# A fused windowed-attention and mixture-of-experts kernel: a new hand-written order, the last unit in two expert halves, end tiles in another PSUM pool

## The chip, the cores and the metric

The kernel runs on one core of a Trainium2 chip. The metric is the device time of one execution in microseconds (us), the median of several runs. A profile of one execution gives the span from the first to the last instruction, and what each engine did: TensorE (PE, its weight loads apart as PEld), VectorE (DVE), ScalarE (ACT), GpSimd (POOL), and SyncE (SP), which only issues DMAs here.

## The reference

There are two stages. The first is attention with 4 batches, 8 heads, 768 positions and head width 64, in which a query sees only the first 8 keys and the last 96, with a linear bias by distance:

```python
keep = is_global | is_local                      # first 8 keys, or 0 <= rel < 96
scores = scale * (q @ k^T) - slopes[h] * dist
a = softmax(where(keep, scores, -1e9));  x = (a @ v) as (B, 768, 512)
```

The second is a layer of 4 attention experts over x. Each expert projects q, k and v (512 to 64), does causal attention over all 768 positions and projects back to 512. A gate picks two experts for each position:

```python
logits = x @ w_gate;  w = softmax(top 2 of logits)
out[pos] = sum over the 2 chosen experts e of  w_e * (causal_softmax(x wq_e, x wk_e) @ (x wv_e) @ wo_e)[pos]
```

The inputs q, k and v have 6.3 MB each, the output has 6.3 MB, all float32.

## The kernel before

The work is cut into 24 units: a unit is 128 positions of one batch, six to a batch (`NU = B * NT`). For each unit there is a fixed set of stages, each a small function, and a string `ORDER` lists all calls of all units, one slot for each. A slot is a stage's two letters, the unit, and, where there is a choice, the engine or queue: `kc5g` casts k of unit 5 on GpSimd (`g`; `v` is VectorE, `a` ScalarE, `s` the SP queue). A loop walks through the string and emits the instructions in exactly that order (`tc.manual_schedule()`), so each engine gets its own instructions as one queue, in the order of the string, and an instruction that waits holds up everything behind it on its engine. The framework sets the semaphores.

The stages, with lines of the kernel before:

- `lk`, `lq`, `lv`: load 256 KB of k, q or v of a unit (L238), on the SP queue or ScalarE's. `wi0` to `wi3` load wk, wq, wv and wo (512 KB each), `wi4` the gate.
- `kc`, `qc` (L258), `vc`, `vx` (L267): cast to float16. `wc` casts weights.
- `tk`, `tq`: transpose k and q on PE (L283), and after q one copy of both out of PSUM (L285).
- `sa`, `sb`: local scores of a unit, bias and scores in one PSUM tile (L345, L352), then the exponential on ScalarE (L355). They need k of this unit and q of this and the next.
- `gs`, `vs`, `vg`, `va`, `vb`: scores of the global keys, and the values (L366, L381); `vb` ends with the normalization on VectorE (L388, L390). `tx` transposes the result (L402).
- `pk`, `pq` (L414), `pv` (L428): the experts' projections. `ro` are the steps of the gate.
- `ca`, `cb`, `cc`: causal scores (L459) and exponentials (L462). `ma` masks the diagonal block on GpSimd (L474).
- `za`, `zb`: causal values of experts 0 and 1, and of 2 and 3 (L487), then on VectorE reciprocal (L494), product with the gate (L496) and scaling (L498). `tz` transposes that (L509, copy L512), `ou` projects it (L519), copies it out of PSUM (L522) and stores 256 KB (L523).
- `xb`, `xm`, `xc`, `xk`, `xs`, `xi`, `az`: masks, biases and zeros made once at the start. `wm5` is five matmuls whose result is never used (L248), which keep TensorE busy. `ck` sums up whether all softmax sums were in a safe range; a branch at the end goes to a slower general path where they were not (not taken here). `bh` marks where the branch may be hinted at.

PSUM has eight banks of 2 KB for each partition. `psS` holds two tiles of two banks (scores), `psZ` one tile of two banks (values), `psT` two tiles of one bank (transposes, projections, outputs). A tile of a pool is given out again when the engines that read it are done. So `za` of a unit can't begin before the scaling L498 of the unit before has read the `psZ` tile.

Of the kernel before, what the change touches and what calls it, by code (L numbers as in the profile page):

```python
# [22 lines left out]
def kernel(  # L23
# [59 lines left out]

    def bias_constants(_):
        V.tensor_copy(rel[:, :], rel_i[:, :])
        ge = const.tile([P, W], F32, name="ge")
        V.tensor_scalar(ge[:, :], rel[:, :], 0.0, None, op0=Alu.is_ge)
        lt = const.tile([P, W], F32, name="lt")
        V.scalar_tensor_tensor(lt[:, :], rel[:, :], float(NL), ge[:, :],
                               op0=Alu.is_lt, op1=Alu.mult)  # L90
        V.tensor_scalar(lt[:, :], lt[:, :], -1.0, -NEG, op0=Alu.add, op1=Alu.mult)
        V.tensor_scalar(rel[KB:P, :], rel[KB:P, :], slopes[1] / slopes[0], None, op0=Alu.mult)
        for p in range(NP):
            V.scalar_tensor_tensor(biasT[:, p, :], rel[:, :], -slopes[2 * p] / sc1, lt[:, :],
                                   op0=Alu.mult, op1=Alu.add)
# [137 lines left out]
    s16s, zs_, x16s, routing, zss, zts, tps, ppss, zs2 = ({} for _ in range(9))  # L233
# [243 lines left out]
    def causal_values(u, i):  # L477
# [6 lines left out]
        z_ps = zs2[u][:, 0, 0:E * VW].rearrange("r (e d) -> r e d", e=E)  # L484
        for e in range(i * E // 2, (i + 1) * E // 2):
            for ci in range(n):
                mm(z_ps[:, e, :], lhsT=a2[:, e % 2, (e // 2) * n + ci, :],  # L487
                   rhs=held("v2buf", b * NT + ci)[:, e, :], start=(e == 0 and ci == 0), stop=True,
                   skip_group_check=True)
# [8 lines left out]
        V.tensor_tensor(zss[u][:, :, :], z_ps[:, :, 0:Hd],  # L498
                        ce[:, :].unsqueeze(2).to_broadcast([P, E, Hd]), op=Alu.mult)

    def turn_z(u, on):
        zts[u] = pp.tile([P, NEP, P], F16, name="zt")
        if on == "s":
            nc.sync.dma_start_transpose(zts[u][:, :, :],
                                        zss[u][:, :, :].rearrange("r e d -> r (e d)"))
            return
        zt_ps = psT.tile([P, NEP, P], F16, name="ztps", tag="t")
# [6 lines left out]
    def output(u, on):  # L514
        b, ri = divmod(u, NT)
        assert 3 in ready
        o_ps = psT.tile([P, D], F32, name="ops", tag="t")
# [5 lines left out]
        dma(out[b, ri * P:(ri + 1) * P, :], o_sb[:, :])  # L523

# [220 lines left out]
    def branch_hint(_):  # L745
# [8 lines left out]
        "vs": (select_values,), "xb": (bias_constants,), "xi": (half_identities,),  # L754
# [9 lines left out]
    }  # L764
    for slot in ORDER.split():
        stage, *args = stages[slot[:2]]
        if slot[-1].isalpha():
            args.append(slot[-1])
        stage(int(slot[2:].rstrip("agsv")), *args)
# [5 lines left out]
    n_f = const.tile([1, 1], F32)  # L775
    V.reduce_sum(n_f[:, :], n_ps[:, :], axis=Ax.X)
    n_i = const.tile([1, 1], I32)
    V.tensor_copy(n_i[:, :], n_f[:, :])
# [13 lines left out]
xb0 lk0s kc0v lq0s az0v az1g lk1s xi0a xs0v xk0g lq1a wm14 tk0 qc0g lv0s kc1g lk2s lq2s lk3a  # L792
wm5 tq0a lq3s xc0g lv1a lv2s lq4s lk4a qc1v lq5s vc0g vx0g wm4 tk1 tq1v xm0v lk5s wm10 sa0 sb0
wm10 vs0 gi0 wi0a wm2 gs0 lk6s kc2v qc2v tk2 tq2v wm3 gs1 lq6s wm7 vg0 kc3g va0 vb0 vc1g vx1v
qc3a sa1 az2g sb1 tk3 tq3v tx0v wi1a vg1 az3g qc4a vc2g kc4g vx2v wm2 va1 wm4 sa2 sb2 vb1 qc5g
gs2 kc5a wc0g tk4 tq4v tx1v az4v lv3s vg2 va2 lv4s vb2 sa3 sb3 tk5 tq5v wm6 tx2v kc6a lq7s wi2a
qc6v wm4 sa4 sa5 tk6 vc3g tq6v pk0 sb4 sb5 wc1v pk1 wm2 gs3 wm2 pq0a vx3v pq1a gi1 vg3 vc4g
vx4g wi4s lv5s va3 vb3 lk7a ca0 ma0 pk2 pq2v tx3v ca1 vg4 va4 vb4 lq8s ca2 pk3 pq3a lk8s vc5v
vx5v cb2 vg5 wc2g lv6s kc7g lq9s pv0v pv1v lq10a lk9s qc7g qc8g kc8g ca3 cb3 tk7 lv7s tq7v pv2v
ro0 va5 sa6 tk8 tq8v tx4v vc6g vx6g lk10a lk11s vb5 sb6 gs4 lv8s ro0 pv3v pk4 qc9g pq4v ro0 ro0  # L800
lq11s lq12a ma1 vs1 lk12s lk13a sa7 tx5v kc9g pv4v kc10g ma2 vg6 va6 ro0 vb6 ca4 tk9 tq9v pk5
lk14s lq13s lv9a pq5v cb4 tx6v sb7 vc7v qc10g qc11a vx7g vc8g tk10 tq10v pv5v kc11g kc12g lq14a
qc12g cc4 vg7 va7 lq15s vb7 ro0 ro0 pk6 pq6a tk11 tq11v vx8g sa8 sb8 tx7v lk15s kc13g kc14g za0
qc13g zb0 lv10a tk12 tq12v gi2 pv6a sa9 sa10 ro1 ro1 lv11s lv12s vc9v vg8 va8 vb8 pk7 pq7a vx9g
tk13 tq13v lk16s lk17s gs5 ca5 qc14g lq16s tz0v za1 lq17s ro1 tk14 tq14v zb1 tx8a ro1 sb9 vc10g
vx10g sb10 kc15a pv7v pv8v vc11g vg9 va9 kc16a vb9 sa11 sa12 tz1v ro1 lq18s kc17v pk8 pq8a za2
ro1 tk15 zb2 sb11 sb12 qc15g tq15v tx9a vc12g vx11g vg10 va10 lk18s vx12g qc16g qc17v vb10 gs6
vs2 tk16 tq16v wi3s qc18g kc18g tk17 tq17v ma3 cb5 vg11 ma4 lk19s va11 lv13s lv14s cc5 tx10v
lv15s tk18 tq18v vb11 ca6 pv9v pv10a ro1 sa13 ro2 sa14 lq19s lq20s gi3 lq21s wc3g za3 ro2 zb3
ou0v ou1a vc13g ro2 ca7 lq22s ca8 vx13g vg12 ma5 va12 vb12 tx11v pk9 pq9v za4 ro2 lk20s kc19g  # L810
zb4 lk21s lk22s lv16s ma6 tz2a ro2 sb13 sa15 tx12v qc19v qc20g pk10 pq10a vc14g vx14g kc20g ma7
tz3v vg13 vc15g ro2 va13 vb13 lv17a cb8 gs7 ma8 ou2v tk19 tq19v lk23s lv18a za5 sb14 sb15 tz4v
zb5 tx13a pv11v sa16 ro2 sb16 vg14 va14 vb14 pk11 ro3 lv19s lv20a pq11a pv12v sa17 za6 zb6 ro3
ro3 vc16g vx15g vx16g ou3a ou4v qc21v ca9 lv21s cb9 tk20 kc21g tq20v za7 pk12 zb7 pq12a tx14v
vc17g ca10 vx17g ro3 cb10 vg15 va15 qc22g tz5v tz6v vb15 ou5a vc18g vc19g tk21 tq21v sa18 vc20v
sb17 kc22g kc23g za8 zb8 tx15a pk13 pq13v ca11 vg16 cc10 va16 pv13v lv22a pv14v cb11 ma9 vb16
gs8 ou6a pk14 pq14v ca12 vx18g vg17 va17 vb17 ca13 tz7v ro3 pk15 ro3 ro3 vx19v pq15a sb18 vs3
tx16v tx17v za9 zb9 ro4 pk16 lq23s pq16a ou7v ro4 lv23s qc23g cc11 vg18 va18 vc21g vb18 pv15a
tk22 tq22v sa19 sa20 ma10 pv16v ma11 za10 tz8a zb10 sb19 sb20 ro4 ro4 ro4 pv17v tz9v ca14 vg19
va19 vb19 ou8a ou9a vx20v sa21 sb21 ro4 ro4 tk23 tq23v ro5 za11 tx18v zb11 tz10a sa22 sb22  # L820
tx19v ma12 pv18v cb14 vg20 va20 vb20 gs9 ro5 ou10a pv19v ma13 vx21g ca15 ca16 vc22g za12 tz11v
zb12 pk17 pq17v pk18 pq18v ro5 ma14 ro5 vc23g cb15 vx22g vg21 va21 vb21 cb16 ro5 tx20v ro5 ro5
pk19 pq19a za13 zb13 pv20a ro6 sa23 sb23 tx21v vg22 va22 vb22 cc16 tz12v pk20 ro6 pq20a za14
zb14 ou11a ro6 ca17 ca18 tz13v ma15 za15 tz14v vx23g zb15 ro6 ro6 ou12a ou13v cb17 vg23 va23
# [46 lines left out]
```

## Time and profile before

| what | value |
|---|---|
| median of 3 runs | 153.25 us (156.71, 151.09, 153.25) |
| the profiled execution's own time | 152.97 us |
| its span, first to last instruction | 150.8 us, so 2.17 us lie around it |
| busy in the span | PE 140.3 us (93%), DVE 111.4, ACT 108.1, POOL 90.2 |
| TensorE's clock | 0.998 of full speed |
| read and written | 20.98 MB and 6.29 MB |

Busy time counts an instruction from its start to its modelled end; PE's matmuls overlap in the pipeline, so a group of them takes less than the sum. The table of stages gives for each stretch the busy time of each engine (with the number of instructions in brackets), TensorE's clock, the mean share of the DMA engines, and GB/s. The chain of waits follows back from the last instruction what released each step. The timeline gives instructions in order of time, with start and duration.

### The profile page before, as it was taken

The page shows a single profiled execution, that of the slowest core. Times are in us where ns is not written, and L with a number is a line of the kernel's source. Part 1 is how long each engine was busy: PE and PEld are TensorE (multiplying, and loading weights), DVE is VectorE, ACT ScalarE, POOL GpSimd, SP SyncE. Part 2 cuts the span into 40 slices and gives each one's busy share as a digit, 9 for nine tenths or more (in the row PEclk, how much of TensorE's full clock was granted, in tenths as well). Part 3 has the DMA queues.
Part 4 walks back from the last instruction along what each step waited for, and adds up shares of the span by engine and source line. Part 5 has one row for each costly group of instructions (what it writes and reads, how often), then busy time and mean ns, then how long its engine had stood idle before and what let it go on. Part 6 is the DMA issues. An engine that isn't in the chain of part 4 may idle for free.

```text
span 150.8 us, 7217 instructions
## 1 busy us (share of the span) xinstructions
PE 140.3 (93%) x3029; PEld 110.2 (73%) x3029; DVE 111.4 (74%) x348; ACT 108.1 (72%) x176; POOL 90.2 (60%) x254
## 2 busy tenths in 40 slices
PE   5799999999999999999978999999999999999760
PEld 4567778887778888878757778888778878786520
DVE  4838676687899887878863987687787777778850
ACT  4027657778576888888638998887977978989640
POOL 7278351568878988797827899136286345463200
PEclk9999999999999999999999999999999999999999
DMA  4999998999999989899899963415221005013462
GB/s 99 280 252 286 276 261 192 254 247 238 277 282 275 245 201 249 189 256 208 231 240 288 301 166 113 116 43 142 74 77 70 4 19 195 24 51 127 155 263 97
DMA packets 85364, 27.77 MB, mean 184 GB/s; under 512 B 82000, under 2 KB 82000, under 8 KB 85328
## 3 DMA queue, kind: packets, MB, share of 16 engines
q1 hardware_dynamic: 62496, 21.51, 56.6%
q10 hardware_dynamic: 22832, 5.77, 17.1%
q8 instruction: 24, 0.39, 1.0%
q14 instruction: 12, 0.10, 0.2%
HBM read 20.98 MB, written 6.29 MB: 181 GB/s over the span
## 4 chain that ended last, share of the span: by engine, by line
PE 74%; DMA 11%; DVE 4%; POOL 3%; ACT 2%; issue 1%; SPq 1%; ACTq 0%; POOLq 0%; DVEq 0%
PE pps L414 14%; PE cps L459 7%; PE vps L428 7%; PE tp L283 7%; PE ops L519 6%; PE zps L487 6%; PE zps L381 6%; PE sps L345 5%; PE zps L248 4%; DMA kf<-in_k_dram 4%; DMA vf<-in_v_dram 4%; PE xps L402 3%; PE sps L352 3%; DMA qf<-in_q_dram 3%; PE zps L366 2%; PE ztps L509 2%
## 5 line engine op out<-in xcount | busy, mean ns | idle before, releaser
L462 ACT ACTIVATE a<-cps 128x1024 f16<-128x1024 f32 (+1 forms) x48 | 42.2, 917 | 8.3 <-PE cps L459 6.6
L355 ACT ACTIVATE abuf<-sps 128x636 f16<-128x636 f32 (+1 forms) x48 | 30.6, 686 | 12.8 <-PE sps L352 10.1
L267 POOL CAST vbuf<-vf 64x256 f16<-64x256 f32 x76 | 31.0, 408 | 8.4 <-DMA vf<-in_v_dram 5.2
L474 POOL TENSOR_SCALAR_AFFINE_SELECT a<-a 128x256 f16<-128x256 f16 x48 | 18.3, 409 | 5.1 <-ACT a L462 4.8
L285 DVE COPY kqT<-tp 128x1024 f16<-128x1024 f16 x23 | 15.7, 688 | 6.6 <-PE tp L283 6.1
L390 DVE TENSOR_TENSOR x<-zps,rinv 128x512 f16<-128x512 f32 x24 | 16.6, 691 | 0.8
L487 PE MATMUL zps<-v2buf,a 128*128 128x65 f16 x336 | 16.0, 193 | 0.6 <-DVE zs L498 0.5
L345 PE MATMUL sps<-biasT,ident 64*64 64x318 f16 (+1 forms) x192 | 14.5, 305 | 1.4 <-ACT abuf L355 1.3
L381 PE MATMUL zps<-vbuf,abuf 64*128 64x65 f16 x704 | 15.5, 189 | 0.0
L258 POOL CAST s16k<-kf 128x512 f16<-128x512 f32 x17 | 10.3, 612 | 8.7 <-DMA kf<-in_k_dram 8.3
L487 PEld LDWEIGHTS <-a 128*128 128x128 f16 x336 | 13.3, 97 | 2.1 <-DVE zs L498 0.9
L381 PEld LDWEIGHTS <-abuf 64*128 64x128 f16 x704 | 14.0, 94 | 1.1 <-issue 0.2
L414 PE MATMUL pps<-xT,wk 128*128 128x128 f16 x192 | 14.7, 219 | 0.0
L414 PE MATMUL pps<-xT,wq 128*128 128x128 f16 x192 | 14.5, 219 | 0.0
L248 PE MATMUL zps<-ident 128*128 128x240 f16 x75 | 12.8, 316 | 1.7 <-POOL ident masks.py:199 1.6
L428 PE MATMUL vps<-wvg,xT 128*128 128x260 f16 x96 | 13.9, 275 | 0.0
L459 PEld LDWEIGHTS <-kq 64*128 64x128 f16 x336 | 9.7, 94 | 5.8 <-issue 4.4
L459 PE MATMUL cps<-kq,kq 64*128 64x128 f16 x240 | 13.8, 218 | 0.0
L519 PE MATMUL ops<-wo,zt 128*128 128x512 f16 x48 | 13.5, 380 | 0.4 <-DVE zt L512 0.4
L352 PE MATMUL sps<-kqT 64*64 64x159 f16 (+2 forms) x384 | 13.8, 223 | 0.0
L258 POOL CAST s16q<-qf 128x512 f16<-128x512 f32 x15 | 9.4, 630 | 5.1 <-DMA qf<-in_q_dram 4.9
L414 PEld LDWEIGHTS <-wk 128*128 128x128 f16 x192 | 11.5, 98 | 0.8
(113 smaller groups left out, 286.4 us busy)
## 6 DMA issues: line engine op xcount, KB each, us to landing
out_dram<-osb SPq DMA_DIRECT2D x24, 256.0 KB, 2.3
qf<-in_q_dram SPq DMA_DIRECT2D x20, 256.0 KB, 5.6
kf<-in_k_dram SPq DMA_DIRECT2D x19, 256.0 KB, 5.7
vf<-in_v_dram SPq DMA_DIRECT2D x17, 256.0 KB, 5.5
vf<-in_v_dram ACTq DMA_DIRECT2D x7, 256.0 KB, 4.7
kf<-in_k_dram ACTq DMA_DIRECT2D x5, 256.0 KB, 4.9
qf<-in_q_dram ACTq DMA_DIRECT2D x4, 256.0 KB, 4.5
w<-in_moe_wk_dram ACTq DMA_DIRECT2D x1, 512.0 KB, 5.3
```

What stands on the lines that cost most here:

```text
L248: mm(current["z"][:, 0, 4 * P - 2 * NC:4 * P].rearrange("r (a n) -> r a n", a=2), lhsT=ident[:, :], rhs=ident[:, 0:NC].unsqueeze(1).to_bro ...
L258: copies[on](s16s[nm, u][:, :, :], fs[nm, u][:, :, :])
L267: copies[on](o[hf * KB:(hf + 1) * KB, c, :, 0:Dh], fs["v", u][c * KB:(c + 1) * KB, hf * HG:(hf + 1) * HG, :])
L345: mm(s_ps[o, hh, 0:2 * w].rearrange("r (c n) -> r c n", c=2), lhsT=ident2[r, :], rhs=biasT[r, p, 0:w].unsqueeze(1).to_broadcast([KB, 2, w] ...
L355: S_.activation(as_[u][:, :, g, :].rearrange("r h (c n) -> r h c n", c=2)[:, :, :, 0:w], s_ps[:, :, 0:2 * w].rearrange("r h (c n) -> r h c ...
L381: mm(zs_[u][:, hf, hq * VW:(hq + 1) * VW], lhsT=as_[u - prev][r, hq % 2, hq // 2, at:at + P], rhs=held("vbuf", u - prev)[r, c, hq, :], sta ...
L414: mm(p_ps[:, i, ep, :], lhsT=w[:, ko, ep, :, :].rearrange("r a d -> r (a d)"), rhs=xT[:, ko, :], start=(i == 0 and ep == 0 and ko == 0), s ...
L428: mm(v_ps[:, :], lhsT=xT[:, ko, :], rhs=wvg16[:, ko, :], start=(ko == 0), stop=(ko == NK - 1))
L459: mm(s_ps[:, e2, i, :], lhsT=kqs[b * NT + ci][r, 0, ep, :], rhs=kqs[u][r, 1, ep, :], start=(i == 0), stop=True, skip_group_check=True)
L462: S_.activation(a2[:, :, 4 * c:4 * c + len(part), :], s_ps[:, :, 0:len(part), :], func=Exp, scale=sc2)
L487: mm(z_ps[:, e, :], lhsT=a2[:, e % 2, (e // 2) * n + ci, :], rhs=held("v2buf", b * NT + ci)[:, e, :], start=(e == 0 and ci == 0), stop=Tru ...
L519: mm(o_ps[:, :], lhsT=zts[u][:, ep, :], rhs=wo16[:, ep, :], start=(ep == 0), stop=(ep == NEP - 1))
```

## The change

There are five edits, and all slots of `ORDER` are in a new sequence.

1. The last unit (23): `za` and `zb` now write the two banks of its `psZ` tile, one for experts 0 and 1 and one for 2 and 3, and each half is divided, weighted and scaled by itself. `tz23` and `ty23` transpose the halves one by one, `ou23` and `oy23` project them, in column halves of 256 each into the two banks of a `psS` tile. The left half is copied by VectorE and stored through the SP queue, the right half copied by ScalarE and stored through ScalarE's queue.
2. `end_tile`: the transposes of units 22 on and the outputs of units 21 on take their PSUM tile from `psS` and not from `psT`.
3. The bias constants come in two parts, `xb` and `xp`, with other work between them.
4. The final sum goes straight to an integer, one VectorE instruction fewer. `bh0` stands first.
5. `ORDER`: the first loads are `v0 q0 k0 q1 k1 k2 k3`, all on SP, and of the 19 loads that ScalarE's queue issued 4 are left. Masks are made before the first casts. There are 64 unused matmuls instead of 75, and they lie elsewhere. Casts and copies change engines here and there.

```diff
+        const_of["lt"] = lt
+
+    def pair_biases(_):
         for p in range(NP):
...
         if i == 0:
             zs2[u] = current["z"] = psZ.tile([P, 2, 4 * P], F32, name="zps2", tag="z")
-        z_ps = zs2[u][:, 0, 0:E * VW].rearrange("r (e d) -> r e d", e=E)
+        last = u == NU - 1
+        nz = E // 2 if last else E
+        z4 = zs2[u][:, :, 0:nz * VW].rearrange("r a (e d) -> r a e d", e=nz)
         for e in range(i * E // 2, (i + 1) * E // 2):
             for ci in range(n):
-                mm(z_ps[:, e, :], lhsT=a2[:, e % 2, (e // 2) * n + ci, :],
...
+                mm(z4[:, e // nz, e % nz, :], lhsT=a2[:, e % 2, (e // 2) * n + ci, :],
...
-        if i == 0:
+        if i == 0 and not last:
             return
...
+        z, e = (z4[:, i], slice(i * nz, i * nz + nz)) if last else (z4[:, 0], slice(0, E))
+        rinv = rinv2[:, b, ri, e]
+        V.reciprocal(rinv, z[:, :, Hd])
+        ce = pp.tile([P, nz], F32, name=f"ce{nz}")
+        V.tensor_mul(ce[:, :], rinv, wts[u // NH][:, ri % NH, e])
+        V.tensor_tensor(zss[u][:, e, :], z[:, :, 0:Hd],
+                        ce[:, :].unsqueeze(2).to_broadcast([P, nz, Hd]), op=Alu.mult)
+
+    def end_tile(u, first, shape, dtype, name):
+
+        if u < first:
+            return psT.tile(shape, dtype, name=name, tag="t")
+        return psS.tile(shape, dtype, name=name, tag="s")
...
-        zt_ps = psT.tile([P, NEP, P], F16, name="ztps", tag="t")
+        zt_ps = end_tile(u, NU - 2, [P, NEP, P], F16, "ztps")
...
-        o_ps = psT.tile([P, D], F32, name="ops", tag="t")
+        o_ps = end_tile(u, NU - 3, [P, D], F32, "ops")
...
+    def turn_last_z(ep, on):
+
+        zt_ps = psT.tile([P, P], F16, name="ztps1", tag="t")
+        nc.tensor.transpose(zt_ps[:, :],
+                            zss[NU - 1][:, 2 * ep:2 * ep + 2, :].rearrange("r e d -> r (e d)"),
+                            ident[:, :])
+        zts[ep, "last"] = pp.tile([P, P], F16, name=f"zt{ep}", bufs=1)
+        copies[on](zts[ep, "last"][:, :], zt_ps[:, :])
+
+    def last_output(ep):
+
+
+        b, ri = divmod(NU - 1, NT)
+        if ep == 0:
+            outs["last"] = [psS.tile([P, 2, D], F32, name="ops1", tag="s")] * 2
+        for i in range(2):
+            c = slice(i * D // 2, (i + 1) * D // 2)
+            o_ps = outs["last"][i][:, i, 0:D // 2]
+            mm(o_ps, lhsT=zts[ep, "last"][:, :], rhs=wo16[:, ep, c], start=(ep == 0),
+               stop=(ep == NEP - 1), skip_group_check=True)
+        if ep == 0:
+            return
+        for i, (copy, queue) in enumerate(((V.tensor_copy, dma), (S_.copy, S_.dma_start))):
+            c = slice(i * D // 2, (i + 1) * D // 2)
+            o_sb = pp.tile([P, D // 2], F32, name=f"osb{i}", bufs=1)
+            copy(o_sb[:, :], outs["last"][i][:, i, 0:D // 2])
+            queue(out[b, ri * P:(ri + 1) * P, c], o_sb[:, :])
...
-xb0 lk0s kc0v lq0s az0v az1g lk1s xi0a xs0v xk0g lq1a wm14 tk0 qc0g lv0s kc1g lk2s lq2s lk3a
-wm5 tq0a lq3s xc0g lv1a lv2s lq4s lk4a qc1v lq5s vc0g vx0g wm4 tk1 tq1v xm0v lk5s wm10 sa0 sb0
-wm10 vs0 gi0 wi0a wm2 gs0 lk6s kc2v qc2v tk2 tq2v wm3 gs1 lq6s wm7 vg0 kc3g va0 vb0 vc1g vx1v
-qc3a sa1 az2g sb1 tk3 tq3v tx0v wi1a vg1 az3g qc4a vc2g kc4g vx2v wm2 va1 wm4 sa2 sb2 vb1 qc5g
-gs2 kc5a wc0g tk4 tq4v tx1v az4v lv3s vg2 va2 lv4s vb2 sa3 sb3 tk5 tq5v wm6 tx2v kc6a lq7s wi2a
-qc6v wm4 sa4 sa5 tk6 vc3g tq6v pk0 sb4 sb5 wc1v pk1 wm2 gs3 wm2 pq0a vx3v pq1a gi1 vg3 vc4g
...
-ma21 pk23 pq23a ro7 za19 zb19 ca22 ou15v tz17v cb22 za20 cc22 tz18v ro7 ro7 ou16a zb20 ou17v
-ck0 ck1 ca23 bh0 cb23 za21 tz19v zb21 ou18v cc23 tz20v ma22 za22 zb22 tz21a ou19a ou20v ma23 za23 tz22v
-zb23 ou21a ou22a tz23v ou23a ck2
+bh0 xb0 xm0v lv0s xk0v xi0a lq0s qc0a lk0s xs0g az0g kc0v wm29 tk0 lq1s lk1s az1v az2g xp0 vc0a
+qc1g lk2s lk3s vx0v kc1g lq2a tq0a kc2v wm12 tk1 tq1v lq3s xc0v kc3g lk4s wm2 vs0 wm9 sa0 sb0
+gi0 lq4s tk2 lv1s qc2g qc3v qc4g lv2s tk3 tq2v gs0 vc1g wm1 tq3v vx1g lq5a gs1 wm3 gs2 vg0 va0
+kc4v vb0 lk5s qc5g wi0s kc5g sa1 sb1 wi1s az3v vc2v lv3a tk4 sa2 vx2g wm4 sb2 tx0a az4v lv4s
+tq4v vg1 wc0g wc1g va1 vb1 wi4s sa3 sb3 wi2s lv5s tk5 lk6s tq5v lq6s lk7s vg2 wm2 va2 vb2 sa4
+sa5 tx1v tx2v lq7s vc3v lq8s gs3 pk0 pk1 vx3v vc4g vx4v lk8s sb4 wm2 pq0a pq1a vg3 vc5g va3 vb3
...
+ro7 ou17v ca23 cb23
+tz19v ma21 za21 zb21 cc23 ou18v tz20v ck0 ck1 ma22 za22 ma23 zb22 tz21a ou19v ou20a za23 zb23
+tz22a ou21a tz23v ou22a ty23v ck2 ou23 oy23
```

## The prediction

> **What bounds the kernel now.** I read the page's busy shares first (PE 93%), then the chain of waits, then the table of stages to see where the missing 7% and the unused matmuls lie, then the timeline of the first 30 us and the last 10.
>
> ```profile
> PE 140.3 (93%) x3029; PEld 110.2 (73%) x3029; DVE 111.4 (74%) x348; ACT 108.1 (72%) x176; POOL 90.2 (60%) x254
> PE 74%; DMA 11%; DVE 4%; POOL 3%; ACT 2%; issue 1%; SPq 1%; ACTq 0%; POOLq 0%; DVEq 0%
> ```
>
> TensorE is the bound: 74% of the chain. Next, the stages (first all work, then the unused matmuls of L248 alone):
>
> ```profile
> 0.00:10.00 10.00, 7.10 (x42) 5.19 (x43) 5.13 (x21) 2.78 (x4) 5.68 (x27) 1.00 0.89 202
> 10.00:20.00 10.00, 9.95 (x198) 7.37 (x197) 7.45 (x19) 5.60 (x11) 6.42 (x16) 1.00 1.25 280
> 20.00:30.00 10.00, 9.68 (x234) 7.96 (x230) 7.46 (x18) 7.36 (x14) 4.29 (x11) 1.00 1.09 229
> 30.00:70.00 40.00, 40.00 (x951) 32.31 (x946) 33.01 (x95) 31.23 (x52) 32.45 (x81) 1.00 1.07 242
> 70.00:80.00 10.00, 8.62 (x205) 7.03 (x203) 7.48 (x22) 5.79 (x11) 5.69 (x16) 1.00 1.01 241
> 80.00:140.00 60.00, 59.88 (x1351) 47.48 (x1351) 46.11 (x155) 51.60 (x81) 34.91 (x104) 1.00 0.38 112
> 140.00:151.00 11.00, 5.07 (x64) 2.83 (x63) 4.77 (x21) 3.75 (x7) 0.77 (x2) 0.97 0.44 165
> ...
> 0.00:10.00 10.00, 5.65 (x26) 3.69 (x27) 1.00 0.89 202
> 10.00:20.00 10.00, 5.01 (x37) 3.04 (x35) 1.00 1.25 280
> 20.00:30.00 10.00, 2.10 (x14) 1.20 (x14) 1.00 1.09 229
> ```
>
> Useful work in the first three stretches is 7.10 - 5.65 = 1.45, 4.94 and 7.58 us. So of the first 30 us TensorE loses 16.0. It loses 1.4 in 70 to 80, and 5.9 in the last 11 us. Between, it is full. Hence the change can earn in three places only, and elsewhere a new order only shuffles full work.
>
> **What the Trainium skill says.** (1) "DMA: Bandwidth & Descriptors", "Issuing engines are not separate DMA queues": DMAs of all issuing engines run on the same 16 DMA engines, and a second issuing engine saves only sequencer time. No stretch of this trace has one queue alone under full load, so it is not shown here; I take it that moving 15 loads from ScalarE's queue to SP costs no bandwidth. (2) Same page, "Anatomy of one DMA": about 2.0 us of a DMA are fixed (stated for another issuing path). The trace agrees in size: the last stores of 256 KB land after 2.0 us. Halving a store therefore saves little. (3) "PSUM — Partial Sum Buffer", "PSUM bank collisions raise a hardware error": two engines must be kept apart on one bank, while different banks are free. In the changed kernel's list of instructions the framework orders by tile, not by bank, as I use below. (4) "TensorE: Matmul & The Clock Gate", "What's actually happening": after an idle window of about 3.4 us the clock falls to half. In every stretch up to 140 us it is 1.00 here, so fewer unused matmuls are safe while gaps stay shorter.
>
> **The start (edits 3 and 5).** Loads: 4.82 MB arrive in the first 20 us (2.02 and 2.80), that is 18.4 tiles of 0.262 MB, some 0.95 us each once running. The old list loads wk (issued at 13.20 us on ScalarE's queue) beside q5 and ahead of k5, and then has no use for wk until 25.87 us; GpSimd meanwhile stands waiting for q5, and later for v3:
>
> ```profile
> 19.38 0.61 POOL L258 CAST s16q<-qf 128x512 f16<-128x512 f32 x1 [2.76 <-DMA qf<-in_q_dram]
> 25.61 0.86 POOL L267 CAST vbuf<-vf 64x256 f16<-64x256 f32 x2 [4.24 <-DMA vf<-in_v_dram]
> 25.87 0.61 PE L414 MATMUL pps<-xT,wk 128*128 128x128 f16 x8
> ```
>
> In the new one q5 and k5 are tiles 14 and 15 (17 us, against 19.4 for q5), wk 16 and 17 (19 us), wq 18 and 19 (21 us).
>
> First scores `sa0`: now 11.03 us. They need k and q of units 0 and 1. New: v0 q0 k0 q1 k1 come in this order, so k1, the fifth, lands near 7.3 (its cast starts at 8.05 now). But VectorE makes the mask first (seven steps, 2.3 us at 10.40 to 12.76 now) and three small memsets, so the cast of k0 moves from 5.21 to about 7. Then tk0, tq0, ScalarE's copy of 1.01, 12 unused matmuls, tk1, tq1, VectorE's copy of 0.69: `sa0` at about 11.3. Price +0.3.
>
> From `sa0` to the first projection L414: 14.84 us now. In that stretch the old list has 38 unused matmuls, the new one 10. Ten of 240 columns take 1.20 us with the last one's tail, 0.1 each. So 28 x 0.1 = 2.8 us of filler go. Whether real work can take the place depends on data: the mask and the cast behind it held tk2 until 13.62 now (VectorE 10.40 to 13.85 without a pause), and that is done beforehand; q5 and k5 come earlier, as said. The useful work before the first L414 is the same but for tk6, tq6 (0.46, now after it) and gs3 (0.25, now before): not a gain, only a shift. From the first L414 to the end of pq1 (3.3 us now) two unused matmuls fewer: 0.2. So by the count 2.8 + 0.2 - 0.3 = 2.7. Following the chain by hand instead (scores of units 1 to 4 at 14.3, 15.4, 17.9 and 19.6 against 16.12, 18.96, 22.11 and 24.82, then L414 when wk is cast at 20 to 21) gives 4.7, without any hitch. From below it is 0, if the waits are just exposed. I take **3.0**. The three ends are kept for the range.
>
> ScalarE loses 15 loads of about 0.4 us of issue each and gains six casts of v (0.35); VectorE and GpSimd keep their load within 1 to 2 us. These engines are at 60 to 74%, so this is worth nothing by itself.
>
> **The middle.** The 1.4 us of 70 to 80 come from this chain:
>
> ```profile
> 61.97 0.28 DVE x L390
> 62.26 5.98 DMA vf<-in_v_dram
> 68.29 0.40 POOL vbuf L267
> ...
> 73.47 4.66 DMA qf<-in_q_dram
> ```
>
> A load of v waits for a buffer, lands 6 us later, and the values wait for its casts. In the new list lv13 to lv15 stand about one unit earlier, but all of them on SP, behind whatever waits there. Between 0 and 1.4 saved; I take 0.5. What is late next is GpSimd, 80% busy in 30 to 70.
>
> **The tail (edits 1, 2, 4).** Counted from the start of the scaling L498 of unit 22, 142.20 now:
>
> ```profile
> 142.20 0.42 DVE L498 TENSOR_TENSOR zs<-zps,ce 128x256 f16<-128x256 f32 x1
> 142.75 0.52 PE L487 MATMUL zps<-v2buf,a 128*128 128x65 f16 x12
> 144.22 0.42 DVE L498 TENSOR_TENSOR zs<-zps,ce 128x256 f16<-128x256 f32 x1
> 145.33 0.29 DVE L512 COPY zt<-ztps 128x256 f16<-128x256 f16 x1 [0.68 <-PE ztps L509]
> 146.32 0.59 ACT L522 COPY osb<-ops 128x512 f32<-128x512 f32 x1 [0.86 <-PE ops L519]
> ```
>
> The last copy ends at 146.91, 4.71 after. New, in the same count: za23 at 0.55, 12 matmuls, reciprocal at 1.11, 0.41 more to the scaling, which takes 0.29 for half the width (0.42 less 128 columns), end 1.81. Now the added wait: zb23 writes the other bank, but of the same tile, and the new list has it wait for VectorE. Behind it are tz22, ou21 and all the rest of TensorE. So zb23 starts at 1.94 (now the two halves follow each other, but for unit 22's transposes); its scaling ends at 3.20. Then tz22, ou21, ou22 (which waits for ScalarE's copy of zt22), ty23 at 3.65, its copy until 4.16; `ck2` on VectorE until 4.5; oy23 done at 4.6; VectorE's copy of 256 columns, 0.42, until 5.05. ScalarE's copy of the other half waits for VectorE's in the new list, again one tile: 0.37, until 5.46. That is 0.75 later. Given back: at most 0.3 by half the store (an estimate from 128 KB at the page's 436 GB/s), and 0.15 for the integer step, which lies beside the store. The waits of 0.2 that edit 2 removes (transposes behind an output copy) are already in this count. `ck0`, `ck1` (1.04 us) stand one unit later, the same on either side of it. `bh0` leaves the branch hint at the same second place in each engine's list: nothing. Price of the tail **+0.5**, between -0.3 and +1.0.
>
> **Sum**, against the profiled execution's own 152.97: -3.0 - 0.5 + 0.5 = -3.0, so 150.0. The median of the runs is 153.25, 0.3 above that execution. A change of about 2% is what a measurement of this kernel can tell from none.
>
> **Rivals.**
> A, the whole chain comes true: 4.7 at the start, 1.4 in the middle, tail 0: 146.9. For it: DMA is at 164 GB/s in 24 to 26 us now, so there is idle transfer to use. Against: TensorE's order is fixed, every hitch counts.
> B, the lead is given back: TensorE reaches batches 1 and 2 earlier than their loads do, and stands where it doesn't now. Start 1.5, middle -0.5 (a loss), tail +0.5: 152.5. For it: DMA share is above 1.0 until 90 us; against: 27 tiles have come by 30 us in both lists, and projections can fill in.
> C, slower: head of the line on SP. All but 4 loads now go through one queue in order, and stores too; a store there waits up to 9.3 us for its copy. The two transfers of the chain above (5.98 + 4.66 = 10.6) cost TensorE only 1.4 today, so 9.2 are covered by other work. If half of the cover (4.6) goes and the early loads stall likewise so that only 0.5 of the start is left: 152.97 - 0.5 + 4.6 + 0.5 = 157.6. It decides from some 3.1 us of new idle time between 40 and 100 us beyond what the start brings.
>
> **Chances.** Forecast 0.40 (its own range 148.4 to 151.5), A 0.15, B 0.28, C 0.17. Faster by over 2% means under 150.2: A, a good half of the forecast, a little of B, 0.44. Slower is C, 0.17. The rest is 0.39. The range goes from A's 146.5 to 154.5, above B, and leaves out most of C.
>
> **What would show it.** Right: first L414 at 22 to 23 us, some 25 unused matmuls between 10 and 30 us; TensorE's useful work up to 30 us near 17 instead of 14.0; in the tail TensorE idle about 0.9 us between za23 and zb23, and the two halves of the last copy one after the other. Wrong: first L414 later than 24.5; more than 2 us of TensorE idle between 30 and 130 (B, C), with POOL or TensorE waiting for loads; or a clock below 1.00 before 30 us.

## The result, and the profile after

The changed kernel takes 172.57 us (median of four runs, 171.36 to 173.95) beside 153.39 for the kernel before. Some executions of either kernel take a few per cent longer than its others, and the ratios here leave those out: 1.131 times as long, 95% interval 1.108 to 1.155. The prediction, 150.0, had the wrong sign. The profiled execution of after took 171.36 us, with a span of 169.7 against 150.8.

From the profile's page of after, first the busy times, then the chain of waits by engine:

```profile
PE 145.6 (86%) x3020; PEld 113.4 (67%) x3020; DVE 113.8 (67%) x359; ACT 109.9 (65%) x182; POOL 89.0 (52%) x241
PE 44%; DMA 25%; SPq 13%; POOL 4%; DVE 4%; ACT 2%; issue 2%; POOLq 0%; DVEq 0%; ACTq 0%
```

TensorE held 74% of the chain before and holds 44% now. Transfers and their issue on SP (DMA, SPq) went from 12% to 38%. So loads hold nearly as much of the chain as TensorE. The stages (columns as before: PE, its weight loads, DVE, ACT, POOL, clock, DMA share, GB/s), then the unused matmuls (`wm`) alone:

```profile
0.00:10.00 10.00, 7.23 (x50) 5.52 (x51) 7.05 (x25) 4.11 (x7) 5.42 (x23) 1.00 1.01 176
10.00:20.00 10.00, 9.10 (x169) 6.29 (x170) 6.05 (x19) 5.89 (x12) 3.37 (x8) 1.00 1.35 220
20.00:30.00 10.00, 8.38 (x175) 6.16 (x175) 6.87 (x18) 4.16 (x7) 5.86 (x14) 0.83 1.08 203
30.00:70.00 40.00, 33.75 (x731) 26.93 (x729) 25.01 (x73) 24.80 (x43) 23.82 (x55) 0.93 0.97 206
70.00:80.00 10.00, 10.00 (x245) 8.64 (x242) 7.13 (x21) 7.38 (x15) 7.46 (x19) 0.95 1.04 230
...
0.00:10.00 10.00, 6.74 (x41) 5.07 (x41) 1.00 1.01 176
10.00:20.00 10.00, 2.81 (x19) 1.57 (x19) 1.00 1.35 220
20.00:30.00 10.00, 0.96 (x4) 0.25 (x4) 0.83 1.08 203
```

Three things stand here. From 30 to 70 us TensorE was full before (40.00) and is idle for 6.25 now, part of the rest at a lower clock. Loads come at 203 to 220 GB/s where they came at 229 to 280. And in 10 to 20 us the DMA engines are *busier* than before (share 1.35 against 1.25) while they move less. The page counts all packets of 16 engines, and nearly all of them hold 256 bytes, so the time of one packet can be worked out: share x 16 x 256 B / rate. That is 18.3 ns before (1.25 x 4096 / 280) and 25.1 ns after (1.35 x 4096 / 220). A packet of the same size from the same tensor has become slower there. From 30 to 70 us, where the engines are less busy, the same sum gives only 19.3 ns after (0.97 x 4096 / 206) against 18.1 before (1.07 x 4096 / 242).

The first projections, awaited at 22 to 23 us, start later than before (timeline of after):

```profile
27.50 1.05 PE L419 MATMUL pps<-xT,wk 128*128 128x128 f16 x16
```

The end, by the timeline: start of unit 22's scaling, second half of the values, the last two copies.

```profile
157.13 0.42 DVE L507 TENSOR_TENSOR zs<-zps,ce 128x256 f16<-128x256 f32 x1
...
158.91 0.52 PE L494 MATMUL zps<-v2buf,a 128*128 128x65 f16 x12 [0.78 <-DVE zs L507]
...
161.42 0.42 DVE L561 COPY osb<-ops 128x256 f32<-128x256 f32 x1 [0.18 <-PE ops L554]
...
161.88 0.37 ACT L561 COPY osb<-ops 128x256 f32<-128x256 f32 x1 [0.64 <-DVE ones L819]
162.15 0.15 DVE L824 TENSOR_REDUCE n_i<-nps 1x1 int32<-1x3 f32 x1 [0.30 <-PE nps L821]
```

Work ends at 162.3. The span ends at 169.7, so 7.4 us follow the last work; before, it was 150.8 - 146.9 = 3.9. Of the 18.9 us that the span grew, 15.4 lie before the last work and 3.5 after it.

### The profile page after: what moved, and what is told of

Read it like the earlier page. It is cut to its first block, busy times and chain, and to the rows that moved or that the text cites. A ratio compares the mean times of both kernels' runs of the same rounds, so it can differ in the third digit from the quotient of the medians.

```text
span 169.7 us, 7189 instructions
## 1 busy us (share of the span) xinstructions
PE 145.6 (86%) x3020; PEld 113.4 (67%) x3020; DVE 113.8 (67%) x359; ACT 109.9 (65%) x182; POOL 89.0 (52%) x241
## 4 chain that ended last, share of the span: by engine, by line
PE 44%; DMA 25%; SPq 13%; POOL 4%; DVE 4%; ACT 2%; issue 2%; POOLq 0%; DVEq 0%; ACTq 0%
SPq L243 11%; DMA qf<-in_q_dram 10%; DMA kf<-in_k_dram 9%; PE pps L419 8%; DMA w<-in_moe_wq_dram 6%; PE ops L530 6%; PE cps L464 5%; PE zps L494 5%; PE vps L433 4%; PE zps L386 4%; PE tp L288 3%; PE xps L407 2%; PE sps L350 2%; PE sps L357 2%; PE ztps L520 1%
## 5 line engine op out<-in xcount | busy, mean ns | idle before, releaser
L272 POOL CAST vbuf<-vf 64x256 f16<-64x256 f32 x66 | 26.6, 403 | 14.7 <-DMA vf<-in_v_dram 8.8
L263 POOL CAST s16q<-qf 128x512 f16<-128x512 f32 x19 | 11.6, 613 | 14.0 <-DMA qf<-in_q_dram 7.7
L386 PE MATMUL zps<-vbuf,abuf 64*128 64x65 f16 x704 | 16.4, 195 | 0.5 <-POOL vbuf L272 0.5
L263 POOL CAST s16k<-kf 128x512 f16<-128x512 f32 x18 | 11.2, 627 | 9.4 <-DMA kf<-in_k_dram 8.2
L386 PEld LDWEIGHTS <-abuf 64*128 64x128 f16 x704 | 15.0, 97 | 1.6 <-issue 1.1
L288 PE MATMUL tp<-ident,s16k 128*128 128x128 f16 x96 | 10.2, 233 | 6.8 <-POOL s16k L263 6.7
L350 PE MATMUL sps<-biasT,ident 64*64 64x318 f16 (+1 forms) x192 | 15.2, 319 | 0.2 <-ACT abuf L360 0.2
L357 PE MATMUL sps<-kqT 64*64 64x159 f16 (+2 forms) x384 | 14.3, 232 | 0.6 <-DVE kqT L290 0.5
L357 PEld LDWEIGHTS <-kqT 64*64 64x64 f16 x384 | 11.7, 111 | 2.0 <-issue 1.0
L288 PEld LDWEIGHTS <-s16k 128*128 128x128 f16 x96 | 6.4, 103 | 9.8 <-POOL s16k L263 8.3
```

The lines of the kernel that those rows point to most:

```text
L263: copies[on](s16s[nm, u][:, :, :], fs[nm, u][:, :, :])
L272: copies[on](o[hf * KB:(hf + 1) * KB, c, :, 0:Dh], fs["v", u][c * KB:(c + 1) * KB, hf * HG:(hf + 1) * HG, :])
L288: nc.tensor.transpose(tps[u][:, i, p, :], s16[:, p * P:(p + 1) * P], ident[:, :])
L357: mm(s_ps[o, hh, c * w:c * w + n], lhsT=kqT[b][r, 0, p, k0:k0 + KB], rhs=kqT[b][r, 1, p, k0:k0 + n], start=False, stop=True, skip_group_ch ...
L386: mm(zs_[u][:, hf, hq * VW:(hq + 1) * VW], lhsT=as_[u - prev][r, hq % 2, hq // 2, at:at + P], rhs=held("vbuf", u - prev)[r, c, hq, :], sta ...
```

## Experiments

Two differences could touch the rate of the loads: the queues (19 loads on ScalarE's queue before, 4 after; none of the 4 is among the 19, which have all gone to SP) and the buffers. The second comes from edit 4. It drops `n_f`, a constant tile of one number, which takes 32 bytes in each partition; all that is allocated after it moves down by 32 bytes. The buffers of k, q and v start at byte 78336 of a partition before, a multiple of 256, and at 78304 after, 224 past one. Below, "on the line" means that the buffers start at a multiple of 256 bytes, "off the line" that they don't.

### The queues alone, and the offset alone

**e1**: the order before, with its 19 `a` loads turned into `s`.

```diff
-xb0 lk0s kc0v lq0s az0v az1g lk1s xi0a xs0v xk0g lq1a wm14 tk0 qc0g lv0s kc1g lk2s lq2s lk3a
+xb0 lk0s kc0v lq0s az0v az1g lk1s xi0a xs0v xk0g lq1s wm14 tk0 qc0g lv0s kc1g lk2s lq2s lk3s
...
```

> The kernel before with one difference: its 19 loads on ScalarE's queue are issued on SP, at the same places of the order. Theory Q (one queue of 256 B packets carries only some 210 GB/s, against 280 for two): loads fall behind as in the changed kernel, 210 GB/s in 10 to 50 us, TensorE starved, 163 to 173 us. Theory O (the new order itself, its places of loads and casts, starves TensorE; the queue is free of cost): 151 to 155 us, 250 GB/s or more in 10 to 50 us.

**e2**: the converse, in the kernel after the same 19 loads on ScalarE's queue again (`lq1a lk3a lk4a lv1a wi0a` ...), and the other 4 on SP.

> The changed kernel with the 19 loads that ScalarE's queue issued in the kernel before back on that queue (and lq2, lq5, lv3, lv21 on SP, as there), in the new order. Theory Q: 150 to 157 us, 250 GB/s or more in 10 to 30 us and the clock back at 1.00. Theory O: 168 to 174 us.

**e5**: the kernel before with the integer sum of edit 4 and nothing else.

```diff
-    n_f = const.tile([1, 1], F32)
-    V.reduce_sum(n_f[:, :], n_ps[:, :], axis=Ax.X)
     n_i = const.tile([1, 1], I32)
-    V.tensor_copy(n_i[:, :], n_f[:, :])
+    with nc.allow_low_precision("whole numbers"):
+        V.reduce_sum(n_i[:, :], n_ps[:, :], axis=Ax.X)
```

> The kernel before with edit 4's integer sum alone, so without the 32 bytes of the tile n_f; that moves every later buffer in SBUF down by 32 bytes, and the buffers that loads fill from a start at 0 to one at 224 modulo 256. Theory A (a 256 B packet written across a 256 B line of SBUF takes 25 ns and not 18, so that all 16 engines carry at most 218 GB/s): 162 to 172 us, 218 GB/s at most in 10 to 50 us. Theory O (the new order of loads and casts): 151 to 154 us, as the kernel before, less 0.1.

Measured: e1 1.081 times the kernel before (1.069 to 1.093), e2 1.152 (1.141 to 1.162), e5 1.086 (1.076 to 1.097). Stages of e1:

```profile
10.00:20.00 10.00, 9.94 (x189) 7.33 (x188) 6.94 (x19) 5.34 (x11) 4.78 (x13) 1.00 0.93 210
30.00:70.00 40.00, 33.24 (x750) 26.44 (x751) 26.58 (x77) 24.07 (x41) 29.17 (x73) 0.99 0.95 213
```

and of e5:

```profile
10.00:20.00 10.00, 9.94 (x147) 7.39 (x144) 6.10 (x16) 4.62 (x10) 6.64 (x18) 1.00 1.35 219
30.00:70.00 40.00, 37.62 (x823) 29.82 (x820) 28.61 (x82) 26.64 (x46) 28.41 (x72) 0.96 1.22 216
```

The two lose about the same time in different ways. In e1 a packet still takes 18.1 ns (0.93 x 4096 / 210), and the engines have gaps: one queue doesn't fill them. Not all of that need be the queue itself. From 30 to 70 us SP waits 8.7 us in sum for buffers to come free, and while it waits no other queue issues; before, it waited 17.1 us, with ScalarE's queue beside it. In e5 the engines are full from 10 to 20 us and a packet takes 25.2 ns; from 30 to 70 us, at a share of 1.22, it takes 23.1. Each fault alone costs 8 to 9%. An edit that removes one VectorE instruction at the very end of the kernel costs 13 us, through an address. And e2 shows why giving the queues back did nothing: the offset was still there.

### The loads by themselves

**e3, e4, e8, e9**: only the 72 loads, each to its own buffer, then 24 stores of zeros; all computation is left out. e3 and e8 issue from SP alone, e4 and e9 alternate; in e3 and e4 the buffers start 128 past a multiple of 256, in e8 and e9 an unused tile of 128 bytes brings them to one.

The first edit makes e4 of e3, the second e8 of e3 and e9 of e4:

```diff
-        issue = nc.sync.dma_start
+        issue = (nc.sync.dma_start, S_.dma_start)[n % 2]
```

```diff
+    pad = big.tile([P, 32], F32, name="pad")
```

> Only the 72 loads of q, k and v, each into a buffer of its own, all on SP, and then 24 stores; all computation is left out. Theory Q: about 210 GB/s while loads run, 18.9 MB in some 90 us. Theory O: 270 GB/s or more, 70 us.

> As the run with loads alone, but every second load is issued on ScalarE's queue. Both theories: 270 to 290 GB/s, 18.9 MB in some 68 us; the difference to the run on SP alone is what theory Q lives by.

> The 72 loads alone on SP (all computation left out), with the buffers at 0 modulo 256 and not at 128. Theory A alone: 18 ns a packet, 280 GB/s, the loads done in 70 us. With a single queue's own limit: 18 ns a packet, 220 to 230 GB/s, 85 us.

> Only the 72 loads, alternating between the SP and the ScalarE queue, then 24 stores of zeros; buffers at a multiple of 256 bytes; all computation is left out. Theory (one queue has a limit of its own, below that of two): 18 ns a packet as on one queue, but 270 to 290 GB/s and not 229 to 250; the loads are done by 72 us instead of 76 to 80, the whole takes 90 to 94 us. Rival (240 GB/s is what loads alone reach, whatever the queues, and the 280 of the kernel before has another reason): 100 us again.

One stretch of each, 10 to 60 us (DVE, POOL, clock, DMA share, GB/s): e3, off the line on one queue,

```profile
10.00:60.00 50.00, 0.00 (x0) 0.00 (x0) 1.00 1.35 218
```

e4, off the line on two queues, has this same line. e8, on the line, one queue:

```profile
10.00:60.00 50.00, 0.00 (x0) 0.00 (x0) 1.00 1.06 240
```

e9, on the line, two queues:

```profile
10.00:60.00 50.00, 0.00 (x0) 0.00 (x0) 1.00 1.28 288
```

In whole times, one run each, 107.66, 107.63, 100.13 and 86.86 us. Off the line a packet takes 25.4 ns, the engines are full, and the queues make no difference. On the line it takes 18.1 to 18.2 ns; then two queues reach 288 GB/s and SP alone 240, with the engines' share at 1.06 of the 1.28 that they can show. In e8 SP issues one load after the other without a pause, some 1.1 us each (262 KB / 240 GB/s), so what limits it lies in that queue and not in the engines. Which part of it (writing the packets, or the number that may be under way) these runs don't tell.

The Trainium skill, "DMA: Bandwidth & Descriptors", "How a descriptor splits into AXI transactions", says of reads that a transaction starts on a 256-byte line, so that a piece which starts off one begins with a transaction from the line below. By that, a single piece of 256 bytes would need two; the page has no such case, and it doesn't speak of writes. The runs agree in direction, and show it where the offset is on the side that is written, in SBUF: with the engines full, 18 ns become 25. That the second transaction is the reason isn't shown; where the engines aren't full, the offset adds only 1 to 2 ns (after from 30 to 70 us, and e12 below).

### Both together, and the change without the offset

**e12**: e1 and e5 together on the kernel before.

> The kernel before with both causes at once: all its loads on SP, and the integer sum alone of the change, so that the load buffers lie 224 bytes past a multiple of 256. Order and tail are those of the kernel before. Theory (both are ceilings on one rate, 218 GB/s and about 230, and the lower one counts): 165 to 169 us, little above either alone; then the kernel after, at 172.6, holds 4 to 7 us of its own order. Rival (the costs add up, 13 each): 176 to 179, and the new order gains 4 to 6 against it.

**e6**: the kernel after, with an unused tile of one number where `n_f` stood. **e7**: the same with the 19 loads of e2 on ScalarE's queue.

```diff
+    pad = const.tile([1, 1], F32)
     n_i = const.tile([1, 1], I32)
```

> The changed kernel with an unused tile of 4 bytes (32 allocated) where n_f stood, which brings the load buffers back to 0 modulo 256; order and queues as in the change. Theory A with a single queue's own limit (225 GB/s as in the kernel before with all loads on SP): 155 to 165 us, packets of 18 ns. Theory A alone: 148 to 153 us, 250 GB/s and more. Theory O: 170 to 174 us.

> The changed order with the 19 loads of the kernel before on ScalarE's queue again, and the load buffers at 0 modulo 256. Theory A with a single queue's limit: 148 to 154 us, 250 GB/s and more in 10 to 30 us, clock 1.00. Theory O: 170 us or more.

Measured: e12 1.124 (1.115 to 1.134), e6 1.099 (1.083 to 1.114), e7 1.092 (1.080 to 1.105); for e7 both expectations failed. So the old order with both faults is about as slow as the changed kernel (1.131, 1.108 to 1.155): 170.25 us beside 172.57. The two don't add up (that would be some 25 us). The last copies of e1, e5 and e12, in this order, show how they combine:

```profile
155.58 0.59 ACT L522 COPY osb<-ops 128x512 f32<-128x512 f32 x1 [0.86 <-PE ops L519]
...
159.97 0.59 ACT L522 COPY osb<-ops 128x512 f32<-128x512 f32 x1 [0.86 <-PE ops L519]
...
161.31 0.58 ACT L522 COPY osb<-ops 128x512 f32<-128x512 f32 x1 [0.86 <-PE ops L519]
```

Before, this copy ends at 146.9. In e1 it ends 9.3 us later, in e5 13.7, in e12 15.0: up to the last work little more than the larger fault counts. The rest of e12, 3.2 us beyond e5, comes after the last work, as does some of e1's loss (see "The time after the last work"). Stages of e12:

```profile
20.00:30.00 10.00, 8.06 (x177) 6.22 (x176) 5.57 (x13) 5.79 (x11) 2.41 (x6) 1.00 0.95 205
30.00:70.00 40.00, 33.83 (x741) 26.60 (x742) 25.52 (x75) 22.09 (x37) 25.26 (x62) 1.00 0.98 202
```

One queue off the line gives 202 to 205 GB/s, less than either fault alone, though a packet takes only 19 to 20 ns here (0.95 x 4096 / 205, 0.98 x 4096 / 202). My expectation of 165 to 169 was too low. And e6, stages:

```profile
10.00:20.00 10.00, 9.74 (x225) 7.37 (x226) 8.31 (x25) 6.50 (x13) 5.06 (x12) 1.00 1.11 250
20.00:30.00 10.00, 9.48 (x211) 6.99 (x210) 6.53 (x19) 5.92 (x11) 4.78 (x13) 1.00 0.98 212
30.00:70.00 40.00, 34.01 (x815) 27.12 (x808) 27.51 (x77) 26.50 (x46) 27.45 (x65) 1.00 0.97 221
```

With the packets fast again the clock is 1.00 up to 70 us and the first projections start at 23.53 us; by 30 us TensorE has done 26.11 - 10.00 = 16.1 us of useful work, against 14.0 before and 14.2 after. The start does bring its 2 us. From 30 us on they are given back at 221 GB/s: TensorE is idle for 6.0 of 40 us. SP waits 14.2 of these 40 us for buffers, so that rate isn't the queue's alone.

### The tail

**e10**: edits 1, 2 and 4 on the kernel before, its order kept up to unit 23 (`bh0` too stays where it was), the buffers held on the line.

```diff
...
-za23 tz22v
-zb23 ou21a ou22a tz23v ou23a ck2
...
+za23 zb23
+tz22a ou21a tz23v ou22a ty23v ck2 ou23 oy23
```

> The kernel before, its order of slots and queues kept up to the last unit, with the new end alone: the last unit in two expert halves, its output by column halves on both queues, the end tiles in the scores' pool, the integer sum. The load buffers are held at a multiple of 256 bytes. Theory (the tail is a small term, as the prediction had it: +0.5, between -0.3 and +1.0): 151.2 to 152.6 beside a kernel before of 151.6. Rival (the serialised halves cost much of what is not yet explained in the aligned kernel after): 155 or more.

Timeline of e10, the same points as above:

```profile
142.61 0.42 DVE L507 TENSOR_TENSOR zs<-zps,ce 128x256 f16<-128x256 f32 x1
...
144.75 0.53 PE L494 MATMUL zps<-v2buf,a 128*128 128x65 f16 x12 [1.07 <-DVE zs L507]
...
147.72 0.37 ACT L561 COPY osb<-ops 128x256 f32<-128x256 f32 x1 [0.60 <-DVE ones L819]
```

From the scaling to the end of the last copy it is 5.48 us (148.09 - 142.61) against 4.71 before: +0.77. The span grew by 0.9. The timed runs give more, 1.016 times (1.008 to 1.025), some 1 to 4 us, above the 151.2 to 152.6 that I had expected. Part of the gap lies in the spans, as that of before belongs to an execution of 152.97, where the ratio compares with 151.4 on average; where the rest lies isn't seen in the profile.

### The staging of the weights

**e11**: the kernel before with two unused tiles, so that the weights' staging buffers lie on the line as well (192 bytes past one otherwise).

```diff
+    pad_w = const.tile([P, 16], F32)
     w32s, ready = {}, set()
...
+    pad_r = big.tile([P, 48], F32)
     raw = fast.enter_context(tc.tile_pool(name="raw", bufs=6))
```

> The kernel before with two unused tiles of 64 and 192 bytes, which bring the weights' staging buffers to a multiple of 256 bytes as well (192 past one in the kernel before) and leave the load buffers at one. The order is that of the kernel before. Theory (256-byte packets to a buffer off a 256-byte line take 25 ns and not 18): the 2.1 MB of weights take about 2 us less of the transfers, and 0 to 2 us of that show: 149.6 to 151.6 beside 151.6. Rival (the weights are hidden): no difference.

1.002 (0.998 to 1.006): no difference. These are two of 21 MB, and what they may gain is hidden.

### The time after the last work

The page lists the fetches of instructions as transfers of their own. In after:

```profile
q14 instruction: 13, 0.11, 0.2%
```

and before:

```profile
q14 instruction: 12, 0.10, 0.2%
```

In after one fetch of 8 KB starts at 168.3 us as the last transfer of the span, 3.7 us behind the one before it. The runs fall into two groups. Where SP has nearly all loads, 6.5 to 7.4 us lie between the last work and the end of the span: e1 6.6, e12 6.8, e6 6.9, e16 6.9, e17 6.5, after 7.4; in each of these such a fetch stands alone, 3.0 to 3.7 us behind the others. Where ScalarE's queue has 18 or 19 loads, it is 3.5 to 3.9 (before, e2, e5, e7, e10, e11, e13, e14, e15, e18), with old and new tail alike, and no fetch inside the span stands alone like that. (e15 counts 13 fetches too, but none of them is late.) SP's list up to the branch at the end has 86 or 87 instructions in those (counted for before, e7 and e18, without the waits for semaphores that stand apart), 101 in after and 105 in e1. The Trainium skill, "Runtime: NRT & Kernel Launch", "Instruction fetch mechanics", says that a taken branch to a page outside the two at hand waits for a fetch. At the end the kernel jumps past its general path, so the split fits a longer SP list that puts the target on another page. That this is the mechanism was not tried apart; that about 3 us come with the loads on SP is what the runs show.

### Is the new order sound when it is fed?

**e13**: e6 with 19 loads on ScalarE's queue in place of 4 (15 more, not the 18 of the expectation), the early ones ahead of casts that wait. **e14**: the same order on the functions of before, with the old tail.

```diff
-bh0 xb0 xm0v lv0s xk0v xi0a lq0s qc0a lk0s xs0g az0g kc0v wm29 tk0 lq1s lk1s az1v az2g xp0 vc0a
+bh0 xb0 xm0v lv0s xk0v lq0a xi0a lq1a lk3a qc0a lk0s xs0g az0g kc0v wm29 tk0 lk1s az1v az2g xp0 vc0a
...
```

> The kernel after, its load buffers at a multiple of 256 bytes, with 18 loads more than it had on ScalarE's queue, the early ones of them set ahead of the casts that wait on that engine (q0, q1 and k3 before the first cast; q2, q4, v2, k5, wk, wq and wv between later steps). Theory (the new order is sound once its loads arrive at 270 GB/s): the clock is 1.00, L414 begins before 24 us, 151 to 155 us, the tail's 0.5 to 2.4 included. Rival (the new order itself is slow, whatever the supply): 160 or more.

> The same order and the same placing of loads as e13, on the functions of the kernel before and with its tail: the last unit in one piece, the old PSUM pools, the old final sum. So only the new order up to the last units and the bias constants in two parts are left of the change. Theory: 0.5 to 2.4 below e13, and beside the kernel before, 3 us of start at the most: 148.5 to 153. Rival (the order is slow): as slow as e13, less the tail.

1.085 (1.069 to 1.101) and 1.079 (1.061 to 1.097). Both theories failed, and the times are those of the rivals, 160 us or more, though from 10 to 30 us the transfers aren't what is short. e13, the stage from 20 us, then two lines of its timeline:

```profile
20.00:30.00 10.00, 5.53 (x116) 4.10 (x116) 4.82 (x12) 4.44 (x8) 5.58 (x16) 0.85 1.29 271
...
23.99 3.61 ACTq L243 DMA_DIRECT2D kf<-in_k_dram  x1
...
28.40 0.51 PE L328 MATMUL gps<-kqT,kg 128*32 128x384 f16 x4 [3.79 <-ACT abuf L360]
```

271 GB/s, and TensorE half idle: ScalarE stood 3.61 us in issuing k7 right behind wv, and its exponentials, which TensorE needed, stood behind that. **e18** spaces these loads some 4 us apart.

```diff
...
-sa5 tx1v tx2v lq7s vc3v lq8s gs3 pk0 pk1 vx3v vc4g vx4v lk8s sb4 wm2 pq0a pq1a vg3 vc5g va3 vb3
...
+sa5 tx1v tx2v lq7s vc3v lq8s gs3 pk0 pk1 vx3v vc4g vx4v lk8s sb4 wm2 pq0a lk7a pq1a vg3 vc5g va3 vb3
...
```

> The kernel after, its load buffers at a multiple of 256 bytes, with 18 loads on ScalarE's queue, spaced some 4 us apart as in the kernel before (q1 and k3 at once, q4, wk, wq, wv, then k7, k10, q12 and so on), and none that waits for a buffer ahead of due work; the rest of the order is that of the change. Theory (supply alone failed): 270 GB/s from 10 to 30 us, clock 1.00, L414 before 25 us, 3.5 us from the last work to the end, 149 to 155 us. Rival (the new order needs its loads in an order and at times that 256-byte packets can't meet on any queues): 160 or more.

1.074 (1.061 to 1.087), still what the rival said. Timeline of e18:

```profile
54.07 0.38 ACTq L243 DMA_DIRECT2D qf<-in_q_dram  x1
...
60.23 0.61 POOL L263 CAST s16q<-qf 128x512 f16<-128x512 f32 x1 [5.98 <-DMA qf<-in_q_dram]
...
64.42 0.61 PE L288 MATMUL tp<-ident,s16k 128*128 128x128 f16 x4 [5.81 <-POOL s16k L263]
```

A load of q that I had set on ScalarE's queue left only at 54.07, when its turn came among ScalarE's own work; GpSimd waited 5.98 for it to land, then TensorE 5.81 for a cast behind it.

**e15, e16, e17** take the small packets out of the question: each load reads 256 KB in one piece, 2 KB for each partition. Other numbers arrive, so the result isn't the kernel's; the amounts and all instructions of the computation stay. e15 is the kernel before, e16 the kernel after with its buffers on the line, e17 the kernel after with them off it.

```diff
-        queues[on](f[:, :, :], {"k": k, "q": q, "v": v}[nm][b, :, ri * P:(ri + 1) * P, :]
-                   .rearrange("h j d -> j h d"))
+        queues[on](f[:, :, :].rearrange("p h d -> p (h d)"),
+                   {"k": k, "q": q, "v": v}[nm][b].rearrange("h j d -> (h j d)")
+                   .rearrange("(t p x) -> t p x", t=NT, p=P)[ri])
```

> The kernel before, in which each load of k, q or v reads 256 KB in one piece (2 KB for each partition) and not 1024 pieces of 256 bytes: other numbers arrive, of the same distribution; order, queues, buffers and all computation stay. Both theories: transfers of 350 to 400 GB/s while they run, the waits for loads shrink, 144 to 150 us.

> The kernel after, its load buffers at a multiple of 256 bytes and its own queues (nearly all loads on SP), with the same wide loads as e15: other numbers of the same distribution arrive. Theory (the new order lost its time to the transfers alone): within 2 us of e15, or up to 3 below it by its shorter start; clock 1.00 throughout. Rival (the new order itself stands in the way, by casts behind one another and loads behind waiting loads): 5 us or more above e15.

> As e16, with the load buffers where the change puts them, 224 bytes past a multiple of 256. Theory (the offset costs a share of a packet that shrinks with the packet's size): at most 1 us above e16. Rival (the offset costs the same share at 2 KB): 5 us or more above e16.

Beside the kernel before: e15 1.008 (1.004 to 1.012), e16 1.002 (0.998 to 1.006), e17 1.014 (1.004 to 1.024). The old order gains nothing from faster loads (I had expected 144 to 150). The new order, fed in this way, is level with it, in spite of the 3 us after its last work. e16, first projections, one stage, and the last work:

```profile
23.59 1.07 PE L420 MATMUL pps<-xT,wk 128*128 128x128 f16 x16
...
30.00:70.00 40.00, 39.89 (x971) 33.16 (x970) 34.40 (x94) 32.90 (x57) 33.07 (x79) 1.00 0.74 269
...
144.22 0.15 DVE L826 TENSOR_REDUCE n_i<-nps 1x1 int32<-1x3 f32 x1 [0.30 <-PE nps L822]
```

and the last work of e15:

```profile
148.20 0.59 ACT L523 COPY osb<-ops 128x512 f32<-128x512 f32 x1 [0.86 <-PE ops L520]
```

Work ends at 144.4 in e16, at 148.8 in e15, at 146.9 in the kernel before. So the new order isn't slow in itself: with wide loads its work ends some 2.5 us before that of the kernel before, which agrees with equal times and 3 us more after the work. Whether the offset still counts at 2 KB a piece stays open: the intervals of e16 and e17 overlap, e17 rests on two runs, and its profiled span is the shorter one (149.6 against 151.3).

## Why the prediction was wrong, point by point

**The steps that failed are two that it set at nothing and one that it never had.**

1. "Moving 15 loads from ScalarE's queue to SP costs no bandwidth" (by count; 19 went, and 4 others came). It was taken from the Trainium skill, "DMA: Bandwidth & Descriptors", "Issuing engines are not separate DMA queues", whose sentence no stretch of the trace could confirm. On the line it is false: 240 GB/s against 288 for loads alone, and 8% of the whole kernel in e1, 3 us of that after the last work. Off the line it is true for loads alone (e3, e4), and nearly so in the kernel, where e12's work ends 1.3 us after e5's. Both queues may well end on the same engines, as the page says; that one queue can fill them doesn't follow.
2. "0.15 for the integer step, which lies beside the store". The instruction is worth nothing, as it lay beside the last copy before (0.14 us from 146.62 us on, where the copy ends at 146.91). Its tile was worth 13 us (e5), as its 32 bytes carried every later buffer off the 256-byte line.
3. The 3 us after the last work come with the loads on SP. The page of before even lists the instruction fetches; no step looked there.

Together, on the old order, the three make 1.124 of the 1.131 (e12). The reverse isn't shown. On the new order, with the buffers on the line and 18 or 19 loads on ScalarE's queue, the third is gone as well, and still 1.074 to 1.092 are left (e7, e13, e18). So the three are enough for the loss, but without them the new order still lost time in each placement of the loads that was tried, and only the wide loads of e16 take that away.

**The start**, -3.0: right in direction, somewhat too large, and lost in the changed kernel. The useful work by 30 us, predicted near 17, was 16.1 in e6 and 16.3 in e16 (25.93 - 9.61), 2.1 and 2.3 above before; the first projections came at 23.5 and 23.6, against 22 to 23. In the changed kernel they came at 27.50, with the clock at 0.83, both named in the prediction as signs that it was wrong.

**The middle**, -0.5: the sign was wrong. TensorE's idle time between 30 and 80 us went from 1.4 to 6.25 us. With wide loads, in e16, it is 0.1 us, so the saving was there to be had.

**The tail**, +0.5: copies and waits came as worked out. TensorE waits 0.78 us between the halves (predicted 0.9; 1.07 in e10), the two last copies follow each other, and the stretch is 0.77 longer in e10 (predicted 0.75), 0.41 in after (5.12 against 4.71). Nothing of the 0.45 that was to be given back is seen: the span of e10 is 0.9 longer. By the timed runs the tail costs 1.2 to 3.8 us, over the +1.0 that the prediction took as its worst, and which of its terms is short isn't known.

**The rivals**: A and B assumed that loads keep their rate. C had the right side and the right resource, but took the order of loads on SP for the cause, and 4.6 us for its price. At the start, where the delay begins, SP does not stand behind waiting stores: in after it issues one load behind the other from 5 to 26 us, mostly 1.1 to 1.3 us each, 4.6 for wq, and is too slow. From 30 to 70 us no store stands there either, but SP waits 13.3 us in sum for buffers (17.1 before), and how much of C's head of the line is in that no run separates. Two readings were slightly off and bear on nothing: the range's lower end is called A's 146.5, where A's sum is 146.9, and B's DMA share "above 1.0 until 90 us" is 0.93 from 60 to 70. **The branch hint**, set at nothing, stays at nothing: it stands first in e13, e14 and e18 too, whose spans end 3.5 to 3.7 us after their work.

What stays open is whether the new order can be fed at 256 bytes a packet. Three placements on two queues (e7, e13, e18) ran at 163 to 166 us. In two of them the waits shown go back to ScalarE, where loads and other work stand behind one another. That may be a fault of the placement, but no placement was found that beats the kernel before, and none of the runs that load the right numbers does.

## What to carry to other kernels

After any change to the allocations, look up where the buffers of small-packet transfers start: a tile of four bytes dropped elsewhere moved them off a 256-byte line here, at 13 us. Work out share x engines x packet size / rate for each stretch; it tells slow packets from a queue that doesn't fill the engines, which need different cures. Before all loads go on one queue, measure that queue alone at the same packet size, and count a longer list of instructions on it as a cost of its own.

## What was unexpected in the hardware

- With the engines full, a packet of 256 bytes into SBUF takes 18 ns on a 256-byte line and 25 ns off it (128 or 224 bytes past one): 288 against 218 GB/s for loads alone (e9; e3, e4). Where the engines weren't full, packets off the line took 19 to 20 ns (after from 30 to 70 us, e12).
- SP's queue alone reaches 240 GB/s with such packets on the line (e8), while the 16 engines reached 288 from two queues (e9). Inside this kernel it moved 213 to 221 (e1, e6, 30 to 70 us), its waits for buffers included.
- Some 3 us more lie after the last work when SP issues 15 to 19 loads more, with a fetch of 8 KB of instructions alone at the end (after, e1, e6, e12, e16, e17).
